# Planning the first chunk's attention in slots 10 to 26 of the weight fold instead of 6 to 24

## Chip, cores and metric

The kernel runs on one core of a Trainium2 chip. The metric is the device time of one execution in microseconds; lower is better. Three runs of the kernel before gave 815.35, 815.65 and 817.64 us, median 815.65.

## What is computed

Causal attention in a window of 64, for 4 sequences of 576 tokens with 8 heads of 64, and after it two feed-forward layers. Everything is float32.

```python
def _attn_ref(q, k, v):
    scores = scale * np.matmul(q, k.transpose(0, 1, 3, 2))
    mask = (rel >= 0) & (rel < 64)
    scores = np.where(mask, scores, -1000000000.0)
    attn = np.exp(scores - np.max(scores, axis=-1, keepdims=True))
    attn = attn / (np.sum(attn, axis=-1, keepdims=True) + 1e-09)
    return np.matmul(attn, v)

def _moe_ref(x, w1, w2, w3, w_out):       # 2304 x 512, inner width 1024
    return ((x @ w1) * (x @ w2) @ w3) @ w_out

def _moe2_ref(x, w_in, w_out):            # inner width 2048
    h = x @ w_in
    return np.maximum(0.01 * h, h) @ w_out
```

## The kernel before, in words

**Precision.** A float32 operand of a large matmul is kept as two reduced-precision halves, high and low. `mm3` (L76) makes one product of three matmuls: high by high (L77), high by low (L78), low by high (L79).

**The fold.** w3 and w_out are multiplied once into one matrix, wf, so that the first layer is ((x w1)(x w2)) wf. This fold is the first stage, from 0 to about 95 us. It runs over two groups `gi` of output rows and eight slices `l` each. `w3_tr` (L466) turns a slice of w3 with TensorE transposes into a PSUM bank (L470), ScalarE casts the high half `w3T` (L472), VectorE subtracts the low half (L473). `w3_mm` (L477) accumulates into the four PSUM banks `mm` of the pool `ps_mm`. After slice 7 of a group the four banks are drained: ScalarE casts (L493), VectorE subtracts (L494). The second group can't write a bank before it is drained.

**Weight units.** Weights arrive as units of up to 1 MB by DMA from SP's queue (`load_unit`, L368) into the buffers `raw` or `wf`, and are turned into usable float32 by ScalarE (L417 scale, L391 low bits) and VectorE (L438 shift, L396 sign). Units 10 to 13 hold w3 for the second group, two slices each; units 14 to 21 hold w1 and w2. For w1, w2 and w_out, `store` (L326) then makes the halves: ScalarE casts (L332), and GpSimd (w1, w2) or VectorE (w_out) subtracts (L333). Units 14 and 15 become `w_104` and `w_105`, the first quarter of w1 and of w2.

**Attention.** It is done in five chunks of blocks of 64 tokens; the first two have six blocks, in two halves of three. A chunk has four head pairs, hence eight half-visits g. The steps of one: `prep_k`, `prep_q` (VectorE transposes, L229, L236), `qk` (TensorE scores `sc` L245; VectorE mask and maximum L249; ScalarE exponential L253), `rn` (row sums, L261, L262; GpSimd scales, L263), `tr` (TensorE transposes L276 into a bank of `ps_ab`, the pool that the w3 transposes also use; ScalarE copies to `pts` L279), and, once per head pair, `av` (TensorE L306; ScalarE and VectorE write the two halves of `x`, L309, L310).

**The stage after the fold.** `ab_step` (L657) multiplies x by w1 and w2 (bank `ab`; ScalarE copies one product, L669; VectorE multiplies, L674). It needs the first chunk's x of all four head pairs. Chunk 1's attention runs beside it.

**What sets the order.** The fold's loop has 16 turns of two slots, 0 to 31; the first group takes slots 0 to 15. `plan_att` (L557) writes the steps of a chunk into a table by slot, and `slot` (L596) writes out what is due:

```python
t0, span, lrn, ltr, lav = STEPS[min(c, 3)]
for j in range(2 * NHP):
    t = t0 + j * span // (2 * NHP - 1)
    pieces = [(-1, 2.5, prep_q, g), (0, 3, qk, g), (lrn, 0, rn, g), (ltr, 2, tp if c > 1 else tr, g)]
    if j % 2:
        pieces.append((lav, 1, av, n))
```

This is only the order in which the program is written. At build, a scheduler with its own model of time reorders the instructions of every engine, attention steps with a raised priority; what it leaves is a fixed order per engine. On the chip each engine issues in that order and waits on semaphores.

Of the kernel before, what the change touches and what calls it, by code (L numbers as in the profile page):

```python
# [21 lines left out]
def tile_kernel(ctx: ExitStack, tc: tile.TileContext, q, k, v, w1, w2, w3, w_out, w_in, w_out2, out):  # L22
# [38 lines left out]
    NF = KF2 // 2  # L61
    YLAG = 1
    RAW = 4
    STEPS = {0: (6, 18, 2, 4, 5), 1: (30, 21, 1, 3, 4), 2: (1, 15, 1, 3, 7), 3: (1, 16, 1, 3, 6)}
    PACED_FROM = 34
    SCALE = 1.0 / float(D) ** 0.5
    act, dve, pool, pe, sp = nc.scalar, nc.vector, nc.gpsimd, nc.tensor, nc.sync
# [489 lines left out]
    def plan_att(c):  # L557

        t0, span, lrn, ltr, lav = STEPS[min(c, 3)]
        if c:  # L560
# [670 lines left out]
```

## Time and profile before

| | us |
|---|---|
| median of three runs | 815.65 |
| the profiled execution, own time | 819.47 |
| its span, first to last instruction | 817.7 |
| TensorE busy | 785.2 |
| VectorE / ScalarE / GpSimd busy | 572.2 / 431.7 / 66.6 |
| TensorE idle before its first instruction | 7.49 |

The profiled execution lies 3.8 us over the median. Windows and timelines below count from the start of its span. A matmul's busy time in the profile is longer than the distance to the next one, since matmuls are pipelined; distances are what adds up.

### The profile page before, as it was taken

The numbers are of one execution on the slowest core, as the hardware profiler recorded it, in microseconds if no ns is written. First come the engines' busy times: TensorE is split into PE (matmuls) and PEld (weight loads), VectorE is DVE, ScalarE is ACT, GpSimd is POOL, SyncE is SP. The second block draws the span as 40 slices with busy tenths as digits, with TensorE's granted clock in tenths as the row PEclk, the third lists the DMA queues.
The fourth block names the chain that finished last, engine by engine and source line by source line (L and its number), as shares of the span: only waits on it lengthen the run. The fifth ranks groups of instructions, "written<-read, shape, count | busy, mean of one in ns | idle before, by whom it ended". The sixth has DMA issues, their size and how long they took to land.

```text
span 817.7 us, 14546 instructions
## 1 busy us (share of the span) xinstructions
PE 785.2 (96%) x5128; PEld 724.6 (89%) x5128; DVE 572.2 (70%) x1349; ACT 431.7 (53%) x964; POOL 66.6 (8%) x61
## 2 busy tenths in 40 slices
PE   5879899999999999999999999999999999999997
PEld 4657699999988888888888899999999999999997
DVE  6995778457456546885731766867767999898976
ACT  6866675344334324443611655654556866575744
POOL 1022434112101100111000000000000000000000
PEclk9899999999999999999999999999999999999999
DMA  9995557347745556888420457998998754444321
GB/s 312 216 267 123 153 165 194 67 98 167 175 105 140 131 133 164 248 256 255 137 64 0 145 176 244 315 330 307 327 322 269 231 171 143 128 132 128 114 94 53
DMA packets 190809, 147.12 MB, mean 180 GB/s; under 512 B 124304, under 2 KB 150160, under 8 KB 190736
## 3 DMA queue, kind: packets, MB, share of 16 engines
q1 hardware_dynamic: 187712, 141.34, 59.1%
q10 hardware_dynamic: 3024, 4.85, 1.6%
q8 instruction: 40, 0.66, 0.3%
q14 instruction: 33, 0.27, 0.1%
HBM read 98.96 MB, written 47.19 MB: 179 GB/s over the span
## 4 chain that ended last, share of the span: by engine, by line
PE 78%; DMA 7%; SPq 5%; ACT 3%; DVE 2%; issue 1%; POOL 0%; ACTq 0%; DVEq 0%
PE ab L77 7%; PE o L78 7%; PE o L79 7%; PE ab L79 7%; PE ab L78 7%; PE o L77 7%; PE pr L77 6%; PE pr L79 6%; PE pr L78 6%; PE mm L78 4%; PE mm L77 4%; DMA raw<-in_moe_w_dram 4%; PE mm L79 3%; PE sc L245 3%; SPq L224 2%; SPq L623 2%
## 5 line engine op out<-in xcount | busy, mean ns | idle before, releaser
L79 PE MATMUL ab<-x,w 128*128 128x512 f32 (+1 forms) x320 | 119.9, 375 | 2.9 <-POOL w L333 2.9
L77 PE MATMUL ab<-x,w 128*128 128x512 f32 (+1 forms) x320 | 119.4, 376 | 2.0 <-ACT x L309 1.1
L78 PE MATMUL ab<-x,w 128*128 128x512 f32 (+1 forms) x320 | 119.9, 375 | 0.0
L77 PE MATMUL pr<-yop,w 128*128 128x384 f32 x300 | 101.5, 338 | 2.5 <-ACT c L826 2.5
L79 PE MATMUL pr<-yop,w 128*128 128x384 f32 x300 | 101.1, 337 | 0.0
L78 PE MATMUL pr<-yop,w 128*128 128x384 f32 x300 | 101.0, 337 | 0.0
L253 ACT ACTIVATE s<-s,nm 128x128 f32<-128x128 f32 x144 | 56.3, 393 | 47.5 <-DVE nm L249 47.5
L826 ACT COPY c<-pr 128x384 f32<-128x384 f32 x95 | 45.1, 479 | 66.2 <-PE pr L79 54.1
L78 PE MATMUL o<-yop,yop 128*128 128x256 f32 x259 | 73.1, 282 | 0.0
L79 PE MATMUL o<-yop,yop 128*128 128x256 f32 x259 | 73.0, 282 | 0.0
L77 PE MATMUL o<-yop,yop 128*128 128x256 f32 x259 | 73.0, 282 | 0.0
L79 PEld LDWEIGHTS ab<-x,w 128*128 128x128 f32 x320 | 60.5, 189 | 10.9 <-POOL w L333 3.2
L77 PEld LDWEIGHTS ab<-x,w 128*128 128x128 f32 x320 | 60.5, 189 | 10.8 <-ACT x L309 1.3
L78 PEld LDWEIGHTS ab<-x,w 128*128 128x128 f32 x320 | 60.6, 189 | 8.2 <-DVE x L310 0.3
L263 POOL TENSOR_TENSOR s<-s,rs 128x512 f32<-128x512 f32 (+1 forms) x40 | 42.4, 1062 | 291.0 <-DVE rs L262 213.1
L829 DVE TENSOR_TENSOR c<-pr,c 128x384 f32<-128x384 f32 x74 | 40.9, 554 | 31.0 <-PE pr L79 19.8
L674 DVE TENSOR_TENSOR p<-ab,a 128x512 f32<-128x512 f32 (+1 forms) x40 | 25.2, 631 | 52.3 <-PE ab L79 39.1
L968 ACT CAST yop<-raw 128x256 fp32r<-128x256 f32 (+1 forms) x92 | 42.4, 485 | 35.5 <-PE o L78 34.8
L78 PE MATMUL mm<-ab,wf 128*128 128x512 f32 (+1 forms) x160 | 59.7, 373 | 0.8 <-DVE ab L676 0.8
L77 PEld LDWEIGHTS pr<-yop,w 128*128 128x128 f32 x300 | 56.4, 188 | 3.8 <-ACT c L826 3.8
L79 PE MATMUL mm<-ab,wf 128*128 128x512 f32 (+1 forms) x160 | 59.3, 371 | 0.0
L77 PE MATMUL mm<-ab,wf 128*128 128x512 f32 (+1 forms) x160 | 56.5, 375 | 0.0
(137 smaller groups left out, 1956.9 us busy)
## 6 DMA issues: line engine op xcount, KB each, us to landing
hd<-c SPq DMA_DIRECT2D x96, 192.0 KB, 4.1
raw<-hd SPq DMA_DIRECT2D x32, 512.0 KB, 3.8
raw<-in_moe_w_dram SPq DMA_DIRECT2D x11, 1024.0 KB, 5.7
raw<-in_moe_w_out_dram SPq DMA_DIRECT2D x18, 512.0 KB, 5.3
raw<-in_moe_w_in_dram SPq DMA_DIRECT2D x16, 512.0 KB, 5.2
wd<-f SPq DMA_DIRECT2D x32, 256.0 KB, 4.1
raw<-wd SPq DMA_DIRECT2D x30, 256.0 KB, 4.4
pd<-tb SPq DMA_DIRECT2D x12, 512.0 KB, 3.0
```

The costliest lines, as they stand in the source:

```text
L77: pe.matmul(ps, lhsT=lh, rhs=rh, start=first, stop=False, skip_group_check=more)
L78: pe.matmul(ps, lhsT=lh, rhs=rl, start=False, stop=False, skip_group_check=more)
L79: return pe.matmul(ps, lhsT=ll, rhs=rh, start=False, stop=last, skip_group_check=more).ins
L224: sp.dma_start(dst, src)
L245: pe.matmul(sc[:, t, :], lhsT=qb[:, t, :], rhs=kT[n][:, k0:k0 + P], start=True, stop=True)
L253: act.activation(out=s[:, t, :], in_=s[:, t, :], func=AF.Exp, bias=nm[:, t:t + 1], scale=-1.0, accum_out=sm[:, t:t + 1])
L263: pool.tensor_tensor(out=s[:, 0:m], in0=s[:, 0:m], in1=rs[:, 0:m].unsqueeze(2).to_broadcast([P, m, P]), op=ALU.mult)
L623: pss["load"] = sp.dma_start(dst, src).ins
L674: dve.tensor_tensor(out=p32, in0=ps, in1=pss["a"], op=ALU.mult)
L826: pss["copy"] = act.copy(self.sb[to], ps).ins
L829: pss["add"] = dve.tensor_tensor(out=self.sb[to], in0=self.ps[at], in1=self.sb[of or to], op=ALU.add).ins
L968: tied("act", lambda: act.copy(out, x))
```

## The change

One row of numbers: chunk 0 starts at slot 10 rather than 6, and its eight half-visits spread over 16 slots rather than 18. The `qk` slots 6, 8, 11, 13, 16, 18, 21, 24 become 10, 12, 14, 16, 19, 21, 23, 26; the `av` slots 13, 18, 23, 29 become 17, 21, 26, 31. The lags within a half-visit and the other chunks' rows stay. No operation is added or taken away.

```diff
-    STEPS = {0: (6, 18, 2, 4, 5), 1: (30, 21, 1, 3, 4), 2: (1, 15, 1, 3, 7), 3: (1, 16, 1, 3, 6)}
+    STEPS = {0: (10, 16, 2, 4, 5), 1: (30, 21, 1, 3, 4), 2: (1, 15, 1, 3, 7), 3: (1, 16, 1, 3, 6)}
```

After the scheduler the engines' orders agree up to TensorE's third group of scores (about 42.8 us in the trace), and SP's up to the load of unit 15. The first place that matters is TensorE at the end of the fold's first group; `w3T_420` and `w3T_384` are slice 7, `mm_592` and `mm_535` the second group's first bank. Before:

```order
L79 MATMUL mm_203<-w_103,w3T_420 128x512
L79 MATMUL mm_207<-w_103,w3T_420 128x512
L79 MATMUL mm_232<-w_103,w3T_420 128x512
L79 MATMUL mm_236<-w_103,w3T_420 128x512
L276 MATMUL ab_499<-ident_94,s_395 128x128 x3
L245 MATMUL sc_609<-kT_564,qbd0_96 128x128 x3
L470 MATMUL ab_557<-ident_94,f_99 128x128 x4
L245 MATMUL sc_676<-kT_564,qbd1_97 128x128 x3
L77 MATMUL mm_592<-w_100,w3T_491 128x512
```

And with the change:

```order
L79 MATMUL mm_203<-w_103,w3T_384 128x512
L79 MATMUL mm_207<-w_103,w3T_384 128x512
L79 MATMUL mm_232<-w_103,w3T_384 128x512
L79 MATMUL mm_236<-w_103,w3T_384 128x512
L245 MATMUL sc_561<-kT_441,qbd1_97 128x128 x3
L470 MATMUL ab_430<-ident_94,f_99 128x128 x4
L470 MATMUL ab_489<-ident_94,f_99 128x128 x4
L77 MATMUL mm_535<-w_100,w3T_429 128x512
```

Two groups of scores and two of transposes that stood ahead of the second group's first matmul now stand behind it (one of the transposes stood earlier, within slice 6's products). So does half of the first head pair's `av`; in exchange half of the fourth pair's `av` moved from before `ab_step`'s first matmul to behind it.

The second place is ScalarE over the same stretch; `wf_123` is the buffer of unit 12, `w3T_491` and `w3T_429` are the second group's first slice. Before:

```order
L253 ACTIVATE s_455,sm_460<-s_455,nm_456 128x128 x3
L472 CAST w3T_491<-ab_492 128x512
L417 ACTIVATE wf_123<-wf_123 128x1024
L391 ACTIVATE wf_123<-wf_123 128x1024
L493 CAST wf_108<-mm_203 128x512
```

And with the change:

```order
L253 ACTIVATE s_510,sm_515<-s_510,nm_511 128x128 x3
L493 CAST wf_108<-mm_203 128x512
L493 CAST wf_108<-mm_207 128x512
L493 CAST wf_109<-mm_232 128x512
L493 CAST wf_109<-mm_236 128x512
L417 ACTIVATE wf_123<-wf_123 128x1024
L391 ACTIVATE wf_123<-wf_123 128x1024
L472 CAST w3T_429<-ab_430 128x512
```

The drain of the banks moved ahead of unit 12's conversion, and the cast of the first slice moved behind it.

The third place is ScalarE at the end of the fold; `x_905` and `x_946` are the x of the fourth head pair, `raw_98` holds units 16 and 17. Before, from the copy that follows unit 16's conversion:

```order
L279 COPY pts_829<-ab_861 128x3x4x32
L332 CAST w_105<-f_99 128x1024
L493 CAST wf_935<-mm_592 128x512
L493 CAST wf_935<-mm_596 128x512
L493 CAST wf_936<-mm_622 128x512
L493 CAST wf_936<-mm_626 128x512
L332 CAST w_106<-f_99 128x1024
L309 CAST x_905<-pa_892 128x384
L417 ACTIVATE raw_98<-raw_98 128x1024
```

And with the change, from one instruction after that copy:

```order
L309 CAST x_823<-pa_810 128x384
L332 CAST w_105<-f_99 128x1024
L253 ACTIVATE s_1026,sm_1031<-s_1026,nm_1027 128x128 x3
L279 COPY pts_849<-ab_895 128x3x4x32
L493 CAST wf_919<-mm_535 128x512
L493 CAST wf_919<-mm_539 128x512
L493 CAST wf_920<-mm_574 128x512
L493 CAST wf_920<-mm_578 128x512
L332 CAST w_106<-f_99 128x1024
L417 ACTIVATE raw_98<-raw_98 128x1024
L391 ACTIVATE raw_98<-raw_98 128x1024
L309 CAST x_946<-pa_933 128x384
```

An x cast, three exponentials and a copy of `pts` entered the stretch, and the fourth x now stands behind the conversion of unit 17 rather than ahead of it. Behind `x_946` come the conversion of unit 18, one more copy of `pts`, and the L669 copy that frees the first `ab` bank; before, that L669 copy came ahead of unit 18's conversion.

On SP's queue, 39 loads of q, k and v stand between the load of `qin` that follows the eight of `kin` and the load of unit 16; before it was 40.

## Rows read from the trace of the kernel before

**Rows 1.** The page, part 1: busy us, share of the span, instructions.

```profile
PE 785.2 (96%) x5128; PEld 724.6 (89%) x5128; DVE 572.2 (70%) x1349; ACT 431.7 (53%) x964; POOL 66.6 (8%) x61
```

**Rows 2.** Windows: length, busy us by engine, granted clock, DMA share, GB/s.

```profile
58.05:94.62 36.57, 36.34 (x234) 29.09 (x235) 24.46 (x71) 23.17 (x64) 9.00 (x8) 0.92 0.56 148
94.62:106.17 11.55, 7.38 (x40) 6.19 (x39) 6.82 (x9) 9.58 (x15) 5.77 (x2) 0.85 0.54 180
...
140.00:160.00 20.00, 20.00 (x160) 19.41 (x160) 8.57 (x37) 8.52 (x29) 2.48 (x3) 1.00 0.37 71
```

**Rows 3.** Timeline of TensorE, 42 to 59 us: start, length, line, idle and releaser.

```profile
44.34 0.55 PE L276 MATMUL ab<-ident,s 128*128 128x128 f32 x3 [1.58 <-POOL s L263]
45.43 0.50 PE L78 MATMUL mm<-w,w3T 128*128 128x512 f32 x1 [0.54 <-DVE w L333]
...
58.05 0.79 PE L77 MATMUL mm<-w,w3T 128*128 128x512 f32 x1 [2.67 <-DVE wf L494]
```

**Rows 4.** Timeline of ScalarE, 53 to 57 us.

```profile
53.97 1.14 ACT L417 ACTIVATE wf<-wf 128x1024 f32<-128x1024 f32 x1 [1.70 <-DMA wf<-in_moe_w_dram]
55.02 1.12 ACT L391 ACTIVATE wf<-wf 128x1024 int32<-128x1024 uint8 x1
56.04 0.56 ACT L493 CAST wf<-mm 128x512 fp32r<-128x512 f32 x1
```

**Rows 5.** DMA issues at 47.8 to 48.5 us, then line L382 up to 120 us.

```profile
wf<-in_moe_w_dram SPq DMA_DIRECT2D x1, 1024.0 KB, 5.8
...
DMA to landing us min/median/max: 3.9/6.9/12.5
```

**Rows 6.** Windows around TensorE's waits; the clock is the third number from the end.

```profile
42.76:45.43 2.67, 0.55 (x4) 0.31 (x4) 2.67 (x3) 0.50 (x1) 1.53 (x1) 1.00 1.21 282
...
58.05:64.15 6.10, 6.10 (x25) 4.57 (x26) 5.60 (x18) 6.10 (x17) 0.33 (x1) 0.50 1.05 386
...
101.48:105.20 3.72, 3.72 (x13) 3.63 (x14) 2.08 (x3) 1.81 (x2) 2.31 (x1) 0.54 0.62 237
```

**Rows 7.** Timeline of TensorE, 80.7 to 82 us.

```profile
80.78 0.49 PE L276 MATMUL ab<-ident,s 128*128 128x128 f32 x3
81.10 0.83 PE L245 MATMUL sc<-kT,qbd 128*128 128x128 f32 x6
81.77 0.27 PE L470 MATMUL ab<-ident,f 128*128 128x128 f32 x1
```

**Rows 8.** Timeline of TensorE after the fold.

```profile
94.62 0.33 PE L77 MATMUL ab<-x,w 128*128 128x384 f32 x1
...
101.48 0.48 PE L79 MATMUL ab<-x,w 128*128 128x384 f32 x1 [2.87 <-POOL w L333]
...
106.17 0.44 PE L77 MATMUL ab<-x,w 128*128 128x384 f32 x1 [0.25 <-ACT a L669]
...
134.54 0.45 PE L78 MATMUL mm<-ab,wf 128*128 128x384 f32 x1 [0.76 <-DVE ab L676]
```

**Rows 9.** Timeline of ScalarE after the fold.

```profile
94.48 1.14 ACT L417 ACTIVATE raw<-raw 128x1024 f32<-128x1024 f32 x1 [3.70 <-DMA raw<-in_moe_w_dram]
...
97.84 2.05 ACT L493 CAST wf<-mm 128x512 fp32r<-128x512 f32 x4
...
100.69 0.52 ACT L309 CAST x<-pa 128x384 fp32r<-128x384 f32 x1
101.06 1.20 ACT L417 ACTIVATE raw<-raw 128x1024 f32<-128x1024 f32 x1
```

**Rows 10.** The page, part 5: the exponentials' row.

```profile
L253 ACT ACTIVATE s<-s,nm 128x128 f32<-128x128 f32 x144 | 56.3, 393 | 47.5 <-DVE nm L249 47.5
```

**Rows 11.** Timeline of SP's queue, then DMA issues at 88.5 to 89.5 us.

```profile
67.60 2.62 SPq L224 DMA_DIRECT2D qin<-in_q_dram  x5
...
88.91 19.37 SPq L382 DMA_DIRECT2D raw<-in_moe_w_dram  x4
...
raw<-in_moe_w_dram SPq DMA_DIRECT2D x1, 1024.0 KB, 5.5
```

## Prediction, made before the changed kernel ran

> **What bounds the kernel now.** I read the page first: TensorE is busy 96% of the span [rows 1], so time is gained or lost where TensorE waits or runs at the low clock. The windows come next. From 140 us on TensorE is full [rows 2], so a shift made in the fold or just behind it is carried to the end almost whole. The stretch to look at is 42.8 to 107 us.
>
> The timeline of TensorE there shows four waits. Two of 1.58 and 0.54 us, on GpSimd's scaling and on the low half of `w_103`, surround one transpose [rows 3]. One of 2.67 us stands ahead of the second group, first matmul at 58.05 us, released by the drain of the first bank [rows 3]. And one of 2.87 us on `w_105` ends at 101.48 us [rows 8]. The last two are followed by 6.10 us at a granted clock of 0.50 and 3.72 us at 0.54, the lower of the two levels (1.2 GHz); in the window of the first two, with the transpose in between, it stayed at 1.00 [rows 6]. ScalarE's timeline tells why the drain was late: it stood behind unit 12's conversion, which waited for a transfer until 53.97 us [rows 4].
>
> **The change, part by part.**
>
> *The waits at 42.8 to 45.4 us.* The transpose that waited for GpSimd goes away from here, but the next matmul needs `w_103`, ready at 45.43 us, and VectorE's order up to there is unchanged. The wait of 1.58 us becomes part of one of 2.67 (0.54 + 0.55 + 1.58). Gain: nothing. The clock may fall behind the longer wait, since it did behind an equal one [rows 3, 6]; but what TensorE does until the next gate below would have room for that.
>
> *The start of the second group.* The drains now stand ahead of unit 12 on ScalarE, so the banks are free early. But the first matmul also needs the cast `w3T_429`, which now stands behind unit 12's two instructions, where before its counterpart stood ahead. Unit 12's load keeps its place on SP's queue and lands 5.8 us after issue [rows 5]; ScalarE starts at 53.97 us, scales until 55.02, makes the low bits until 56.04 [rows 4], and casts w3T in as long as it casts a drained bank, 0.56: start at 56.6 us. Against 58.05 that is 1.45 us earlier. The wait itself is longer than before: TensorE leaves the first group at about 50 to 51 us.
>
> *The work that moved behind that point.* Two groups of scores and two of transposes: 0.67 us each (81.10 to 81.77) and 0.32 each (80.78 to 81.10) [rows 7], together 1.98 us. The halves of `av` cancel. The stretch before took 36.57 us, 36.34 of it busy [rows 2], so TensorE sets its pace: first matmul of `ab_step` at 94.62 - 1.45 + 1.98 = 95.15 us, against 94.62 [rows 8]. VectorE and ScalarE were busy 24.46 and 23.17 us in it [rows 2], which leaves room for two half-visits more.
>
> *The end of the fold.* Here ScalarE is the gate. Before, from 94.48 us it worked without a pause until the fourth x was cast at 100.69 [rows 9]. The beginning is unit 16's landing, 5.5 us after its issue at 88.91; ahead of it SP issued 40 loads from 67.60 on, 0.53 us each [rows 11]. Now there are 39: issue at 88.4, start on ScalarE at 93.95. From there I add in the new order:
> - unit 16, one copy and `w_105`'s cast, as before: 97.84 - 94.48 = 3.36 [rows 9];
> - the third x ahead of them, 0.37 (100.69 to 101.06 [rows 9]);
> - three exponentials, 3 x 0.393 = 1.18 [rows 10], and a copy of `pts`, by the x cast 0.37;
> - the four drains and `w_106`'s cast, 100.69 - 97.84 = 2.85 [rows 9];
> - unit 17, 56.04 - 53.97 = 2.07 [rows 4], and the fourth x, 0.37: x ends at 104.5 us;
> - unit 18, 2.07; a copy, 0.37; the L669 copy, 0.37: 107.35 us.
>
> The L669 copy frees the bank for the matmul that started at 106.17 us before [rows 8]. So that point comes 1.2 us later, and the 0.5 us of the step before is hidden under it, as is the wait for `w_105`, since GpSimd gets its cast at about the same time. If SP were held up as little as the row allows the other way, by none of the 0.53 gained, the point lies at 107.9; if unit 16 is issued as soon as its buffer is free, some 3.5 us earlier by the order of VectorE, it is bounded by TensorE instead, at about 106.2.
>
> *The clock behind it.* Before, the low stretch ended by 105.20 us [rows 6]. Now TensorE gets its work between 101 and 107 us in pieces, with waits for the third and fourth x. No row shows pieces like these. From below it costs nothing; from above, a further 6.10 us at half speed behind 107.35 costs 3.05 [rows 6]. The nearest row is the 3.72 us after the wait for the same weights, worth 1.86; I take half of it, 0.9, because the low stretch partly runs while TensorE would wait anyway.
>
> *Later.* The wait of 0.76 us at 134.54 [rows 8] may shrink or double. I take nothing.
>
> **Sum:** 1.2 + 0.9 = 2.1 us. On the profiled execution: 817.7 + 2.1 = 819.8 us of span. That execution was 3.8 us over the median; the difference carries over, so 815.65 + 2.1 = **817.7 us**. A measurement of this kernel can tell some 0.3%, 2.45 us, from no change; the forecast is within that.
>
> **The rivals.**
>
> *The early drain pays (faster).* The wait ahead of the second group was a wait for a bank [rows 3]; if it goes with its low-clock stretch, 2.67 + 6.10 / 2 = 5.7 us are gained: 810.0 us. It needs `w3T_429` soon after the drain, so unit 12 on ScalarE by about 52 us, under 3.9 us from its issue, the smallest landing on that line [rows 5], and unit 16 earlier too. A part of it, from SP's side alone, gives some 2 to 3 us. The Trainium skill ("Perfetto Trace Analysis", section "Matmuls") has it that matmul groups should rotate through PSUM banks so that the draining of one overlaps the next group's matmuls; by that rule the drain is what holds the second group, and the sum would be the 5.7 us of this case. The trace agrees only for before: the order of ScalarE puts another operand of the same matmul behind the transfer. Chance 0.13.
>
> *The clock stays low and the fourth x is the new gate (slower).* Place: TensorE between 101 and 113 us. Price: 1.2 + 3.05 = 4.25 us, 819.9 us; with unit 16 not earlier, 0.5 more. It decides for this side once the low clock lasts 2.5 us beyond 107.35 us. For it: both waits of over 2.6 us were followed by it [rows 6], and ScalarE has no pause in which to catch up. Against it: 3.72 us were enough last time. The sum of my forecast is so near the bound that this case takes much: chance 0.38.
>
> *It hardly does what it says (no change).* The first three groups of scores don't move at all, since the scheduler places them as before; what moves is hidden under the transfers of units 12 and 16, and chunk 1 absorbs the rest: 815.7, up to 0.5 either way. Chance 0.14.
>
> **How the numbers follow.** The forecast, 0.3 to 2.4 us slower, has 0.35; with the third rival that is 0.49 within 0.3%. Slower 0.38, faster 0.13. The range reaches down to half of the gain of the first rival, 815.65 - 2.85 = 812.8 us, and up to the second with the half microsecond and the 0.76 us of the later wait: 815.65 + 5.5 = 821.2 us.
>
> **What would show it.** Right: ScalarE's L493 drains near 50 to 52 us, unit 12's L417 still near 54, the second group's first matmul at 56 to 57 us, released by ScalarE's L472; the first `ab_step` matmul within a microsecond of 95; the fourth x cast after 104 and the L669 copy near 107. Wrong: a start of the second group before 55 us or a first `ab_step` matmul before 93.5 (then VectorE and ScalarE gave more than I counted), new waits of over a microsecond on VectorE inside the second group (then the pace there wasn't TensorE's), or a different pattern of waits beyond 140 us, which I took as unchanged.

## Result and the profile after

| | before | after |
|---|---|---|
| median of ten executions | 815.74 us (814.07 to 817.64) | 820.18 us (817.17 to 822.38) |
| profiled execution, own time | 819.47 | 817.17 |
| its span | 817.7 | 815.4 |

The change makes the kernel slower: ratio 1.0051, interval 1.0034 to 1.0067, some 4.4 us. The forecast was 817.7 us; the range of 812.8 to 821.2 holds the result.

The two profiled executions stand the other way round: that of before, at 819.47 us, lies above all ten of its kernel, that of after is the shortest of its ten. Laid side by side they show the changed kernel 2.3 us ahead, so they can't show where 4.4 us went. The experiments therefore begin with further traces of both kernels. What the first trace of after does show is the order of events.

The page of after, part 1, answers to [rows 1]; the work is the same:

```profile
PE 785.5 (96%) x5128; PEld 725.5 (89%) x5128; DVE 575.7 (71%) x1349; ACT 431.8 (53%) x964; POOL 66.2 (8%) x61
```

The timeline of TensorE at the wait for `w_103` and at the start of the second group, to be held against [rows 3]:

```profile
44.21 0.50 PE L78 MATMUL mm<-w,w3T 128*128 128x512 f32 x1 [2.65 <-DVE w L333]
...
53.80 0.79 PE L77 MATMUL mm<-w,w3T 128*128 128x512 f32 x1 [3.20 <-ACT w3T L472]
```

The two waits around one transpose have become one, and the second group starts 9.59 us behind it (before 12.62), now released by the cast L472. ScalarE's timeline, against [rows 4], tells why:

```profile
48.41 2.06 ACT L493 CAST wf<-mm 128x512 fp32r<-128x512 f32 x4 [2.08 <-PE mm L79]
51.15 1.12 ACT L417 ACTIVATE wf<-wf 128x1024 f32<-128x1024 f32 x1 [0.68 <-DMA wf<-in_moe_w_dram]
52.17 1.12 ACT L391 ACTIVATE wf<-wf 128x1024 int32<-128x1024 uint8 x1
53.17 1.06 ACT L472 CAST w3T<-ab 128x512 fp32r<-128x512 f32 x2
```

The drains run as soon as the products are there, and the cast then stands behind unit 12's conversion. Behind the fold, against [rows 8], TensorE:

```profile
93.18 0.34 PE L77 MATMUL ab<-x,w 128*128 128x384 f32 x1
...
97.64 0.45 PE L79 MATMUL ab<-x,w 128*128 128x384 f32 x1 [0.81 <-POOL w L333]
...
101.03 1.01 PE L77 MATMUL ab<-x,w 128*128 128x384 f32 x2 [1.89 <-ACT x L309]
102.76 0.90 PE L276 MATMUL pa<-ident,s 128*128 128x128 f32 x3 [0.72 <-DVE x L310]
...
104.87 0.69 PE L77 MATMUL ab<-x,w 128*128 128x384 f32 x1
```

The wait for `w_105` shrank from 2.87 to 0.81 us; in its place TensorE waits for both halves of the fourth x. The second half is VectorE's (L310), and on VectorE too unit 17 now stands ahead of it, with its shift L438; before, the subtraction came first (101.52 and 103.38 us in the first trace):

```profile
100.70 1.54 DVE L438 SCALAR_TENSOR_TENSOR f<-raw 128x1024 int32<-128x1024 int32 x1 [0.50 <-issue]
102.16 0.54 DVE L310 TENSOR_TENSOR x<-pa,x 128x384 fp32r<-128x384 f32 x1
```

On ScalarE, against [rows 9]:

```profile
90.29 1.13 ACT L417 ACTIVATE raw<-raw 128x1024 f32<-128x1024 f32 x1 [3.10 <-DMA raw<-in_moe_w_dram]
...
98.41 1.19 ACT L417 ACTIVATE raw<-raw 128x1024 f32<-128x1024 f32 x1
...
100.46 0.51 ACT L309 CAST x<-pa 128x384 fp32r<-128x384 f32 x1
100.82 1.25 ACT L417 ACTIVATE raw<-raw 128x1024 f32<-128x1024 f32 x1
...
103.75 0.48 ACT L279 COPY pts<-pa 128x384 f32<-128x384 f32 x1 [0.67 <-PE pa L276]
104.34 0.48 ACT L669 COPY a<-ab 128x384 f32<-128x384 f32 x1
```

The three L417 rows are units 16, 17 and 18. The fourth x stands behind unit 17, the L669 copy that frees TensorE's bank behind unit 18. And the window of low clock there, against the last of [rows 6] (3.72 us at 0.54):

```profile
100.41:107.24 6.83, 5.49 (x16) 4.55 (x17) 6.46 (x7) 5.45 (x9) 2.15 (x2) 0.50 0.32 99
```

### The profile page after: what moved, and what is told of

It reads as the page before. It is cut to its first block, busy times and chain, and to the rows that moved or that the text cites. A ratio compares the mean times of both kernels' runs of the same rounds, so it can differ in the third digit from the quotient of the medians.

```text
span 815.4 us, 14548 instructions
## 1 busy us (share of the span) xinstructions
PE 785.5 (96%) x5128; PEld 725.5 (89%) x5128; DVE 575.7 (71%) x1349; ACT 431.8 (53%) x964; POOL 66.2 (8%) x61
## 4 chain that ended last, share of the span: by engine, by line
PE 82%; DVE 5%; DMA 5%; ACT 4%; SPq 2%; issue 1%; ACTq 0%; POOL 0%; DVEq 0%; POOLq 0%
PE o L78 7%; PE o L79 7%; PE o L77 7%; PE ab L77 7%; PE ab L78 7%; PE ab L79 7%; PE pr L77 7%; PE pr L79 7%; PE pr L78 7%; PE mm L77 5%; PE mm L78 5%; PE mm L79 5%; PE sc L245 3%; PE pa L306 2%; DMA raw<-in_moe_w_dram 2%
## 5 line engine op out<-in xcount | busy, mean ns | idle before, releaser
L77 PEld LDWEIGHTS ab<-x,w 128*128 128x128 f32 x320 | 60.6, 190 | 11.1 <-ACT x L309 2.2
```

The source lines that it names most:

```text
L77: pe.matmul(ps, lhsT=lh, rhs=rh, start=first, stop=False, skip_group_check=more)
```

## Experiments

The kernel before took between 815.85 and 816.12 us beside these runs.

### More traces of both kernels

No edit. 

> The kernel before, unchanged, for a second trace of it on the chip of the next three runs. All theories expect 814 to 818 us, ratio 1.000 within 0.2%. What is looked for: where in the first 110 us its timeline of TensorE differs from the first trace, and by how much (the first trace was of its slowest execution, 3.8 us over the median). If the luck of the first loads is the reason, the wait for the first group's last weights (ended at 45.43 us before) ends 1 to 4 us earlier here and all that follows is shifted alike.

> The changed kernel, unchanged, for a second trace of it. Expected: 819 to 822 us, ratio 1.003 to 1.008. Theory A (end of the fold): the loss of 4.4 us against the kernel before lies between the first ab_step matmul and 115 us, as waits for the third and fourth x, for w_105 and a low clock of 6 us or more; first ab_step matmul no later than before, within 1 us. Theory B (second group's start): the first ab_step matmul already comes 3 us or more later than in the kernel before on this chip, after a wait of over 3.5 us for the cast L472 behind unit 12's transfer. Theory C: neither place, the loss lies behind 140 us, where the two timelines drift apart by 2 us or more.

> The kernel before, unchanged, for a third trace. The first trace had a stretch of low clock behind the fold (101.5 to 105.2 us), the second had none. By the granted clock of its other executions the usual one has about 14 us at the low clock in all, as the second: no low stretch between 93 and 110 us, and the first L669 copy about 10 us after unit 16's conversion begins.

Measured: before_again 817.08 us (ratio 1.0014, interval 0.9998 to 1.003), its trace of 815.37; before_third one execution of 814.84; after_again 820.02 us (1.005, 1.0033 to 1.0068), its trace of 819.88. So before_again and after_again are traces of executions near their kernels' medians, and their spans differ by 4.5 us.

From 170 us on the traces of the two kernels keep a constant distance but for some 0.5 us, so what counts lies in front of that. The stretch that differs in every pair is the one from unit 16's conversion on ScalarE to the first product of `y_step` (`mm` from `ab` and `wf`) on TensorE. Windows over it, in before_again:

```profile
91.92:106.61 14.69, 11.73 (x75) 10.42 (x73) 10.81 (x15) 13.47 (x19) 6.81 (x3) 1.00 0.54 168
```

in before_third:

```profile
91.93:107.75 15.82, 12.96 (x73) 11.52 (x72) 11.04 (x15) 13.57 (x19) 7.01 (x3) 0.89 0.48 162
```

and in after_again:

```profile
91.85:112.08 20.23, 16.68 (x94) 13.82 (x92) 18.07 (x25) 16.90 (x28) 11.21 (x5) 0.83 0.58 195
```

Unit 16 arrives at the same time in all three; the first y product is then 4.3 to 5.5 us later in the changed kernel. Read in the same way from every trace (us; the last column is the granted clock of the stretch):

| trace | own time | unit 16 starts | first L669 copy ends | first y product | whole stretch | clock |
|---|---|---|---|---|---|---|
| before, first | 819.47 | 94.48 | 106.12 | 110.69 | 16.21 | 0.89 |
| before_again | 815.37 | 91.92 | 102.03 | 106.61 | 14.69 | 1.00 |
| before_third | 814.84 | 91.93 | 103.00 | 107.75 | 15.82 | 0.89 |
| after, first | 817.17 | 90.29 | 104.82 | 110.48 | 20.19 | 0.83 |
| after_again | 819.88 | 91.85 | 106.38 | 112.08 | 20.23 | 0.83 |
| x_first | 818.62 | 90.96 | 104.49 | 109.06 | 18.10 | 1.00 |
| hold_17 | 816.72 | 91.90 | 103.80 | 108.39 | 16.49 | 1.00 |
| span_only | 820.11 | 92.41 | 107.59 | 114.64 | 22.23 | 0.69 |

Before the mean is 15.57 us, after 20.21: 4.6 us, which is the whole of the loss within what executions differ by. Two things keep this from being a measure of lost time alone. The stretch holds more of TensorE's work in the changed kernel, 93 and 94 instructions against 69 to 75, since the second group now ends later against unit 16 and half of the fourth pair's `av` moved into it. And about 1 us comes back behind it: from the first y product to the end the changed kernel takes 704.9 and 706.0 us, before 705.3 to 707.0. The like comparison is hold_17 (last row but one), with 92 instructions in the stretch. Theory A (the end of the fold) stands; B and C fall: after_again's first `ab_step` matmul was at 94.73 us, 1.3 later than in before_again, and behind 140 us nothing is added. Two details of the expectations missed: the first `ab_step` matmul is not within 1 us, and before_third does have 3.4 us of low clock behind the fold, so an execution of before near the median has it or not.

### The fourth x ahead of unit 17 (x_first)

`issue_after` queues an instruction behind another on its engine. `W12` is 14, so the condition holds for units 17 and up.

```diff
-        act.copy(x[:, 0, 0:W * m], pa)
+        pss["x", n] = act.copy(x[:, 0, 0:W * m], pa).ins
...
+                with tc.issue_after(pss["x", 3]) if now["scale"] >= W12 + 3 else nullcontext():
                     act.mul(u["hi"].bitcast(F32), u["hi"].bitcast(F32), 2.0 ** -112)
                     low_bits(u["raw"])
```

> The changed kernel with one order undone: on ScalarE the cast of the fourth x stands ahead of the conversions of units 17 and 18, as it did before. Theory A: the fourth x is cast 2.07 us earlier, TensorE's wait ahead of it goes, and 2 to 4 us of the 4.4 come back: 816.5 to 818.5 us. Theory B or C: within 0.7 us of the changed kernel, about 820.

Measured: 819.77 us (1.0046, 1.0031 to 1.0062), no gain over the changed kernel. Its ScalarE timeline:

```profile
99.08 0.53 ACT L309 CAST x<-pa 128x384 fp32r<-128x384 f32 x1
99.45 1.24 ACT L417 ACTIVATE raw<-raw 128x1024 f32<-128x1024 f32 x1
...
101.55 1.20 ACT L417 ACTIVATE raw<-raw 128x1024 f32<-128x1024 f32 x1
...
103.95 0.54 ACT L669 COPY a<-ab 128x384 f32<-128x384 f32 x1
```

and two rows of its TensorE:

```profile
104.54 0.44 PE L77 MATMUL ab<-x,w 128*128 128x384 f32 x1 [1.91 <-ACT a L669]
...
123.02 0.55 PE L276 MATMUL pa<-ident,s 128*128 128x128 f32 x3 [1.31 <-POOL s L263]
```

The x came 2 us earlier and the two conversions then stood, one behind the other, ahead of the L669 copy: the wait passed from the x to the bank. The stretch shrank by 2.1 us all the same, at full clock, in the shortest execution of its eight; but from the first y product to the end this run took 707.8 us, 1.8 to 2.9 more than the changed kernel, 1.31 of it a new wait for GpSimd at 123 us. The expectation failed because it followed one gate and not the next ones.

### The first casts ahead of unit 12 (cast_first)

`until(n, stop)` writes conversions out until unit n is done, and none from unit `stop` on; with 12 in place of `W12`, that is 14, unit 12's is written later.

```diff
-        act.copy(both[:, 0], ps.rearrange("p i k -> p (i k)"))
+        pss["cast"] = act.copy(both[:, 0], ps.rearrange("p i k -> p (i k)")).ins
...
+                with tc.issue_after(pss["cast"]) if now["scale"] == 12 else nullcontext():
                     act.mul(u["hi"].bitcast(F32), u["hi"].bitcast(F32), 2.0 ** -112)
                     low_bits(u["raw"])
...
-                until(last["w3", g2, l2], W12)
+                until(last["w3", g2, l2], W12 if g2 and l2 else 12)
...
-                until(last["wo", l2 - 1], W12)
+                until(last["wo", l2 - 1], 12)
```

> The changed kernel with the cast L472 of the second group's first two slices ahead of unit 12's conversion on ScalarE, behind the four drains, so that no transfer holds the start of the second group. That start should come at 51.5 to 53 us instead of 56 to 57, the wait ahead of it falls from over 3 us to 1 or less. Theory B: 3 to 5 us faster than the changed kernel, 815 to 817 us. Theory A: what is won at the start is lost again at the end of the fold, where ScalarE waits for unit 16's transfer: within 1 us of the changed kernel, 819 to 821 us.

Measured: 819.88 us (1.0045, 1.0028 to 1.0062), as theory A said. TensorE:

```profile
51.17 0.50 PE L77 MATMUL mm<-w,w3T 128*128 128x512 f32 x1 [0.40 <-ACT w3T L472]
...
93.69 0.64 PE L77 MATMUL ab<-x,w 128*128 128x384 f32 x1 [4.13 <-ACT pts L279]
```

and the rows of ScalarE that its second wait goes back to:

```profile
91.19 1.10 ACT L417 ACTIVATE raw<-raw 128x1024 f32<-128x1024 f32 x1 [7.78 <-DMA raw<-in_moe_w_dram]
...
93.18 0.46 ACT L279 COPY pts<-ab 128x384 f32<-128x384 f32 x1
```

The group started 6.8 us after the wait for `w_103` instead of 9.6 to 11.3. Nearly all of it came back as one wait (this trace is of an execution 2.3 us under the run's median): ScalarE stood 7.78 us idle before unit 16's transfer, with a copy of `pts` that TensorE needed behind it in the queue. The Trainium skill ("PSUM — Partial Sum Buffer", section "Engine vs sequencer instructions") calls ScalarE's queue a strict FIFO; these rows agree, since the copy ran only at 93.18 us, behind unit 16's two instructions.

### Units 17 and 18 where they were (hold_17)

The hold of x_first for unit 17, and unit 18 written after the first `ab_step` and queued behind its L669 copy (`pss["copy"]`):

```diff
+                with (tc.issue_after(pss["copy"]) if W12 + 4 <= now["scale"] < PHASE_B else
+                      tc.issue_after(pss["x", 3]) if now["scale"] == W12 + 3 else nullcontext()):
...
-    until(W12, PHASE_B)
+    until(W12, W12 + 4)
...
-                    advance(PHASE_B)
+                    advance(PHASE_B if i else W12 + 4)
```

> The changed kernel with only the orders of units 17 and 18 undone: unit 16's conversion stays ahead of the attention's last steps, unit 17's stands behind the cast of the fourth x (as in the run x_first), and unit 18's behind the first L669 copy. In x_first the gate only passed on to that copy, which stood behind both conversions (1.91 us of wait). If the price is what stands behind unit 16 up to the L669 copy, the fourth x comes 2.07 us and the copy some 3 us earlier than in the changed kernel: 816.5 to 818.5 us, between it and the run with unit 16 held as well (816.4). If unit 16's own place is what counts: 819.5 us or more.

Measured: 816.18 us, ratio to the kernel before 1.001 (0.9996 to 1.0024): the loss is gone, though the interval leaves room for up to 2 us of it. ScalarE:

```profile
100.01 0.51 ACT L309 CAST x<-pa 128x384 fp32r<-128x384 f32 x1
100.38 1.18 ACT L417 ACTIVATE raw<-raw 128x1024 f32<-128x1024 f32 x1
...
103.31 0.48 ACT L669 COPY a<-ab 128x384 f32<-128x384 f32 x1
103.69 1.17 ACT L417 ACTIVATE raw<-raw 128x1024 f32<-128x1024 f32 x1
```

and the whole stretch:

```profile
91.90:108.39 16.49, 14.02 (x92) 11.41 (x91) 13.79 (x23) 15.35 (x27) 7.64 (x4) 1.00 0.46 157
```

20.2 us became 16.5, and the granted clock of the stretch rose from 0.83 to 1.00. The attention steps are still as late as in the changed kernel, and still stand behind unit 16. Chunk 1's order behind it changed too, but from the first y product to the end hold_17 takes 706.5 us, no less than the changed kernel (704.9 and 706.0), so the gain lies ahead of that product. What cost the time is the place of two conversions. Much of it took the form of low clock: over all executions the mean granted clock is 0.9929 in hold_17 (12) and 0.9885 in the changed kernel (16), by which up to 3.6 us, nearly all that was won, are TensorE's clock. That is an estimate: twice what is missing from 1 times the span is the time at 1.2 GHz, and half of the difference is lost if TensorE had work in it.

### The shorter span alone (span_only), and with the hold (span_hold)

span_only starts at slot 6, as the kernel before, with the changed kernel's span of 16; the edit is shown against the changed kernel. span_hold adds the hold of units 16 and 17 that the next section describes.

```diff
-    STEPS = {0: (10, 16, 2, 4, 5), ...
+    STEPS = {0: (6, 16, 2, 4, 5), ...
```

> One half of the change: the attention starts at slot 6 as before and spreads over 16 slots (6 to 22) instead of 18. Up to the first group's end the order is that of the kernel before, so the second group starts behind the drain at about 12.6 us after the wait for w_103, as before. Theory A: the steps of the fourth head pair come earlier, none is added behind unit 16 on ScalarE; the loss is gone and the time lies within 1.5 us of the kernel before, 814 to 817 us. Rival (the shorter span crowds the second group): VectorE waits appear inside the second group and the time is near the changed kernel's, 818 to 821 us.

> The attention in slots 6 to 22 (the run span_only, 819.7 us) with units 16 and 17 held back on ScalarE as in the run hold_16. In span_only no attention step is late, but unit 17's conversion stood ahead of the fourth x and unit 18's, waiting 3.45 us for its transfer, ahead of the first L669 copy. If the place of the conversions is the cause and the slots themselves matter little, this comes to the level of the kernel before with the same hold (814.1): 813 to 816 us. If the shorter span costs by itself: 818 us or more.

Measured: span_only 819.68 us (1.0037, 1.002 to 1.0053), span_hold 816.22 (1.0012, 0.9999 to 1.0024). The first expectation of theory A failed, for a reason that its ScalarE timeline shows:

```profile
97.70 1.14 ACT L417 ACTIVATE raw<-raw 128x1024 f32<-128x1024 f32 x1
...
100.72 0.47 ACT L309 CAST x<-pa 128x384 fp32r<-128x384 f32 x1
104.64 1.19 ACT L417 ACTIVATE raw<-raw 128x1024 f32<-128x1024 f32 x1 [3.45 <-DMA raw<-in_moe_w_dram]
...
107.07 0.52 ACT L669 COPY a<-ab 128x384 f32<-128x384 f32 x1
```

Here no attention step was late, yet the scheduler again put unit 17 ahead of the fourth x and unit 18, which waits for a transfer, ahead of the L669 copy. On VectorE unit 17's shift stands ahead of the x's other half, and that is TensorE's longest wait here:

```profile
101.89 2.44 DVE L438 SCALAR_TENSOR_TENSOR f<-raw 128x1024 int32<-128x1024 int32 x1
104.25 0.54 DVE L310 TENSOR_TENSOR x<-pa,x 128x384 fp32r<-128x384 f32 x1
...
104.84 0.90 PE L276 MATMUL pa<-ident,s 128*128 128x128 f32 x3 [2.59 <-DVE x L310]
```

The rival has the time but not the place: TensorE has no wait inside the second group. TensorE's clock there:

```profile
99.40:113.00 13.60, 9.62 (x30) 8.11 (x29) 12.58 (x14) 8.31 (x12) 6.74 (x3) 0.50 0.59 199
```

With the conversions held back 3.5 us return; that is a little above the 813 to 816 us expected. It ends 2.1 us above the kernel before with the same hold (814.08, next section; 3.0 us by the two ratios, since they were measured beside different runs of before). What makes that rest, the shorter span or the order that the scheduler made of it, no run shows.

### Unit 16 held back too (hold_16, cast_hold, before_hold, before_cast_hold)

hold_16 is hold_17 one unit earlier: unit 16 behind the fourth x, unit 17 behind the L669 copy (`W12 + 2` and `W12 + 3` in place of `W12 + 3` and `W12 + 4`). cast_hold adds the edit of cast_first. before_hold and before_cast_hold are the same edits in the kernel before.

> The changed kernel with the conversions of units 16 and 17 moved back on ScalarE: unit 16's stands behind the cast of the fourth x, unit 17's behind the first L669 copy. In the second trace of the changed kernel unit 16 landed at 91.85 us and 10.2 us of work stood behind it up to the fourth x (before: 6.2). Theory A (the ScalarE chain behind unit 16's landing sets the end of the fold): w_105's cast comes near 92 us instead of 94.7, the fourth x near 98 instead of 102, the first L669 copy near 101 instead of 105.9, and no wait of over 1 us is left there; 3 to 5 us faster than the changed kernel, 815 to 817 us, if w_106 and w_107, now later, don't stop TensorE near 108 to 112 us. Rival (the clock alone): the granted clock falls between 100 and 107 us whatever the order, since the second group starts after the same wait; 819 to 820.5 us.

> Both edits together in the changed kernel: the first two slices' casts ahead of unit 12's conversion, and units 16 and 17 held back as in the run before. With the casts first alone the second group started at 51.2 us and its last product ended at 89.6 us, but TensorE then waited 4.13 us for a copy that stood behind unit 16 on ScalarE. Theory A: that wait goes too, and the 3 to 5 us won at the start are kept: 811 to 814.5 us, faster than the kernel before. Rival: w_104 and w_105 become the gate instead, since units 14 and 15 arrive no earlier; then a wait of 2 to 4 us for a w on GpSimd's L333 stands at 90 to 94 us and the time is 815 to 818 us.

> The kernel before (slots 6 to 24) with units 16 and 17 held back on ScalarE in the same way. If the chain behind unit 16 costs the kernel before too, its wait of 2.65 us for w_105 near 98.9 us shrinks below 1 us: 813 to 814.5 us. If w_105 is late for another reason, such as GpSimd's own queue, 815 to 817 us.

> The kernel before with both edits: unit 12 behind the drains and the first cast, units 16 and 17 held back. With the hold alone the second group still started at 57.9 us, 13.1 us after the wait for w_103. If the gains add as they did in the changed kernel (816.4 to 813.6), the start comes at 52 to 54 us and the time is 810 to 813 us. If the start gained is taken by the attention steps that then stand between the groups: 813.5 to 815 us.

| | us | ratio to before | interval |
|---|---|---|---|
| hold_16 | 816.36 | 1.0002 | 0.9981 to 1.0022 |
| cast_hold | 813.62 | 0.9974 | 0.9958 to 0.999 |
| before_hold | 814.08 | 0.9975 | 0.9958 to 0.9992 |
| before_cast_hold | 817.69 | 1.0022 | 1.0007 to 1.0036 |

Two of them are faster than both kernels. before_hold did what was expected of it: the wait for `w_105`, 2.65 to 2.87 us in the three traces of before, is gone from its trace, so the kernel before paid for the same queue too. hold_16 shows what the whole queue costs, and that not all of it can be had. Its TensorE from the first `ab_step` matmul to the first y product, a window of 10.89 us against 17.30 in the first trace of after (93.18 to 110.48):

```profile
93.86:104.75 10.89, 10.59 (x79) 9.56 (x78) 9.25 (x14) 9.15 (x15) 2.87 (x3) 1.00 0.22 66
```

and its waits later:

```profile
100.23 0.45 PE L77 MATMUL ab<-x,w 128*128 128x384 f32 x1 [0.30 <-ACT a L669]
...
129.73 0.44 PE L78 MATMUL mm<-ab,wf 128*128 128x384 f32 x1 [2.42 <-DVE ab L676]
...
140.17 0.44 PE L78 MATMUL mm<-ab,wf 128*128 128x384 f32 x1 [0.97 <-DVE ab L676]
```

From the first y product to the end of the span hold_16 takes 711.1 us, hold_17 706.5: the 3.6 us by which it is ahead at that product, and a little more, are given back behind it. These waits stand there, and a granted clock of 0.60 from 142.2 to 145.7 us behind them; that they are the whole of it no run shows. In cast_hold the start is kept as well; its second group begins 8.4 us after the wait for `w_103`, and no wait for unit 16 follows:

```profile
52.12 0.53 PE L77 MATMUL mm<-w,w3T 128*128 128x512 f32 x1 [0.40 <-ACT w3T L472]
...
96.23 0.44 PE L77 MATMUL ab<-x,w 128*128 128x384 f32 x1 [0.30 <-ACT a L669]
```

In the kernel before the two edits don't add, against the expectation. The second group did start where it was expected, at 53.75 us; but the same order on another plan came with a new gate on VectorE; before_cast_hold's TensorE:

```profile
76.03 0.88 PE L276 MATMUL ab<-ident,s 128*128 128x128 f32 x3 [4.13 <-DVE w3T L473]
```

and VectorE ahead of that L473:

```profile
74.78 0.38 DVE L236 STREAM_TRANSPOSE qbd<-qin 64x192 f32<-64x192 f32 x1 [0.63 <-DMA qin<-in_q_dram]
75.19 0.69 DVE L473 TENSOR_TENSOR w3T<-ab,w3T 128x512 fp32r<-128x512 f32 x1
```

A step of the fold stands behind transposes of q that wait for their loads: by this trace the same fault, in another queue. Behind the wait the granted clock is 0.54 for 5.97 us. No run takes that order out again, so this cause is read and not tested.

## Why the prediction was half right

**The waits at 42.8 to 45.4 us: right.** One wait of 2.65 us, nothing gained. That the clock may fall behind it is also seen: it did in after_again and not in the first trace.

**The start of the second group: right as to the gate and the distance.** Forecast 11.2 us behind the wait for `w_103` (56.6 less 45.43); measured 9.59, 11.28, and 10.12 to 11.67 in the runs that share this order up to there, against 12.62 to 13.11 in the traces of before. The releaser is the one named, the cast behind unit 12's transfer. The absolute times missed: by the prediction's own signs of being wrong the first trace of after is past both (start at 53.80 us, before 55; first `ab_step` matmul at 93.18, before 93.5), the second past neither (55.39, 94.73). The reason given beside those signs is not what the rows show: unit 12 was on ScalarE at 51.15 us rather than 53.97 in the first trace and at 52.75 in the second, so the transfer came earlier. The first rival, that the early drain pays, is out for the reason given against it: the drain was early, but it no longer held the start. By the rule of the Trainium skill that it drew on ("Perfetto Trace Analysis", section "Matmuls") the time would have been 810.0, an estimate from this case's rows. In cast_first the group began while later banks were still being drained, as that rule wants (its next bank came 0.77 us late, at 53.12 us, from VectorE's L494), and nothing was gained, since the end of the fold had another gate.

**The moved work: undersized, and hidden as said.** Forecast 1.98 us. From the group's first matmul to the first of `ab_step` it took 39.38 and 39.34 us, against 36.57 in the first trace of before and 36.08 in before_again: 3.0 (before_third, 34.91, had half their low clock there). The two short rows that it was priced from [rows 7] lie well behind the low stretch [rows 6]. It decides little: hold_17 has the same work there and is back at the time of before.

**The end of the fold: right mechanism, wrong size.** This is the step that failed: "that point comes 1.2 us later". The chain itself was exact to the fourth x: 10.2 us from unit 16's start forecast, 10.17 and 10.18 measured. Two things were off behind it.
- From unit 16's start to the end of the L669 copy I had 13.4 us; both traces have 14.53. The copy of `pts` between the two waits for TensorE's transposes ([0.67 <-PE pa L276]), which wait for the fourth x's other half themselves ([0.72 <-DVE x L310]) and run at the low clock. I added ScalarE's durations as if nothing could come back from TensorE.
- I set it against 11.7 us, from a trace 3.8 us over the median whose TensorE stood at the low clock just there [rows 6, 8]. The other two traces have 10.1 and 11.1. Part of the harm that the change does was already in the baseline, and I took the change as costing only what it adds to a bad execution. The row of that trace that told it: ScalarE's copy ahead of the L669 copy waited 1.97 us for TensorE, against 0.47 in before_again, so ScalarE alone was not the gate there:

```profile
105.26 0.48 ACT L279 COPY pts<-pa 128x384 f32<-128x384 f32 x1 [1.97 <-PE pa L276]
```

Together 14.53 - 10.94 (the mean of the three) = 3.6 us instead of 13.4 - 11.7 = 1.7, of which the earlier issue of unit 16 took 0.5. That half microsecond isn't seen: unit 16 starts at 91.92 and 91.93 us in two traces of before and at 91.85 in after_again.

**The clock: right.** From the L669 copy to the first y product it took 5.66 and 5.70 us, before 4.57 to 4.75: 1.05 against 0.9. More of the clock's price sits in the point above. Over all executions the mean granted clock is 0.9885 after (16) and 0.9912 before (98); twice what is missing times the span is 18.8 and 14.4 us at 1.2 GHz. Half of that difference, 2.2 us, is the clock's share of the loss, if TensorE had work in that time. The clock is only one form of it: cast_first has a mean of 0.9911, that of before, and is no faster than the changed kernel; there the wait of 4.13 us stands in its place.

**Later: right within a microsecond.** From the first y product to the end 704.9 and 706.0 us, before 705.3 to 707.0.

**The sum.** 3.6 + 1.05 = 4.65 us against 2.1; the time says 4.4. The two agree better than they must, since about 1 us comes back behind the first y product and the traces scatter by more than the difference. The second rival had the place and, at 4.25 us, nearly the price: fourth x and low clock between 101 and 113 us. My chance of 0.38 for it was too low, because the forecast and it differed by how bad the one baseline was, which took more traces to tell. That the range holds the result is this rival's doing: its upper end was the rival's price, and 2.5 us lie between the forecast and the measured time.

## What to carry to other kernels

In a queue that runs in order, work that can wait (a conversion for a weight needed later, above all one whose transfer is still under way) belongs behind the instruction that frees a bank or an operand for the busiest engine; hold it there explicitly, since moving the surrounding work can reshuffle what the scheduler puts first, as in span_only. When one such gate is removed, read on to the next, in the same queue and in the others: x_first moved the wait from an operand to a bank and gained nothing, and before_cast_hold came with a new wait on VectorE. And before a stretch of one trace is used as a baseline, look whether that execution lost time in it: a profile 0.5% over the median hides effects of that size.

## What was not expected of the hardware

A wait of nearly the same length was followed by the low clock in one execution and not in another. In the first trace of after TensorE went on at full clock after 2.65 us; in after_again, after 2.57 us, the window behind the wait reads

```profile
44.11:47.26 3.15, 3.15 (x8) 2.48 (x8) 3.09 (x12) 3.15 (x8) 0.00 (x0) 0.50 0.92 162
```

And shorter waits, or waits as long, came with far longer low stretches: 6.83 us in after, where the clock fell during the 1.89 us for the fourth x, and 13.60 us in span_only, where waits of 1.98, 0.77, 2.59 and 0.61 us followed one another. In hold_17, with waits of 0.81, 1.11 and 0.29 us in that stretch, it didn't fall. What sets the one from the other these runs leave open.
